# A delta-rule recurrence and an MLP mixer in one kernel: the joins of batch element 0 in 32x32 tiles, with identity products that assemble the blocks in PSUM, and a new order of all steps

## The chip, the core and the metric

The kernel runs on one core of a Trainium2 chip. The metric is the device time of one execution in microseconds (us). The engines are TensorE (PE, with its weight loads PEld), VectorE (DVE), ScalarE (ACT), GpSimd (POOL) and SyncE (SP, which issues all DMAs here). Everything is computed in fp32. Each product of the program shows in the trace as two PE records, except a transpose, which shows as one; counts of records below are therefore mostly twice the counts of products.

## What is computed

```python
# q, k, v: (4, 8, 768, 48), beta: (4, 8, 768)
k_n = k / (norm(k) + 1e-6)
for t in range(768):                       # for each batch element and head
    y[t]  = q[t] @ state                   # state: 48 x 48
    v_old = state @ k_n[t]
    state = state + beta[t] * outer(k_n[t], v[t] - v_old)
x = y as (4, 768, 384)                     # heads side by side
h = relu(x^T @ w_tok1) @ w_tok2            # mixing over the 768 tokens
u = x + h^T
out = u + relu(u @ w_ch1) @ w_ch2          # 384 -> 1536 -> 384
```

## The kernel before, in words

**Units.** The recurrence is done in chunks of 64 time steps (`C`). Two chunks of all 8 heads make a *unit* u of 128 steps; a batch element has 6 units (`NCH`), so there are 24. Units 0 to 5 are batch element 0, and only they take the paths with `u < NCH`. Inside a chunk the steps are solved together, which needs the inverse of a unit triangular 64x64 matrix per head and chunk. A unit holds its eight pairs of them in `gm` (the trace also calls the places of units 0 and 1 `wc`), 128 partitions by 8 blocks (`NB`) of 176 columns; the 64 columns `TC` are the triangular matrix, first as it is and then inverted in place.

**From a unit to its inverse.** `load_kq` (k), `prep` (p) and `grams` (c, d) load k and q, turn them on PE (L488, L507; evicted by ACT at L491, L511) and build the matrices (products L442, DVE L445). `to_parts` (t, L598 on ACT, L603 on DVE, L605 on POOL) copies the diagonal 32x32 blocks of a unit into one tile `xins` for a round of up to four units; `invert` (i) inverts all blocks of a round on DVE. In batch element 0 DVE inverts only the 16x16 diagonal blocks (L676, L680) and then transposes them back twice with 32x32 block transposes: the left 16 columns into `t16` (L686), all of it into `xins` (L693).

**The joins of batch element 0.** Two stages of products make the 64x64 inverse out of 16x16 and 32x32 blocks. `join_16` (h) first forms `p_z` from the untouched matrix and `t16` (L710, 16 products per unit with 64-row, 64-column weights and 32 columns), so that `t16` must hold the blocks of even and of odd quarters in two column halves, with zeros elsewhere: ACT scales a copy by `odd` (L687) and DVE scales it by `even` (L688). ACT evicts `p_z` into `z` in two copies scaled by `sides` (L716). Then `from_parts` (f) writes the inverted diagonal blocks back into `gm`: ACT for all rows, scaled by `even` (L622), DVE (L629) and POOL (L632) for the odd quarters. A second set of 16 products (L725, 48 weight columns) gives the 16x16 corner blocks, which ACT puts in place in four copies of 16 partitions (L731). `join` (j) does the same for 32 to 64: a DVE transpose into `t11` (L749), 16 products (L773), two ACT copies into `zst` (L778), 16 products with 33 weight columns (L760), two ACT copies of 32 partitions into `gm` (L754). The later batch elements go through DRAM and the same `join`, with the second set of products of a unit interleaved with the first set of the next.

**The recurrence.** `recur` (r) has 48 steps, 12 (`NQ`) for each batch element. Step t waits for step t-1 through PE, DVE and ACT: products of the state (L813), DVE subtraction (L820), products (L833, L837), the ACT copy `w_t` (L843), products (L851, L852), the DVE update of the state (L860, first one L862) and the ACT copies of the result into `xb` (L865). Step r0 needs unit 0 joined.

**The mixer.** `mixer` (m) of a batch element begins when its steps are written: token mixing (L1009, L1022), turns (L1032), then the channel MLP in pairs of chunks (L1089 for batch element 0, the faster algorithm L981 with 15 products per pair of blocks for the others, L1111 for the second matrix).

**The order.** The program is recorded under a manual schedule: each function is a generator, and a string `order` of about 2,700 steps (`h0*4` is four steps of `join_16(0)`) says in which order they are recorded. Each engine executes its own instructions strictly in that order. Three kinds of steps are only there to keep PE busy: `x` and `z` multiply zeros by zeros into an unused PSUM tile `p_warm` (128x128 weights and 128 or 512 columns, L227), `y` and `Y` the same in 64x64 tiles (L237).

Of the kernel before, what the change touches and what calls it, by code (L numbers as in the profile page):

```python
# [8 lines left out]
FP32 = mybir.dt.float32  # L9
# [14 lines left out]
def kernel(  # L24
# [508 lines left out]
    for n in (2 * QB * RU * NB,):  # L533
        cuts.append(cuts[-1] + n)
    t16 = spare[:, cuts[1] : cuts[2]].rearrange("s (q t b) -> s q t b", q=2, t=QB)
    borrowed = {}

    def z_of(u):
        if not borrowed:
            borrowed["z"] = mlp_pool.tile(  # L540
                [128, NCH, NB * (C - QB)], FP32, name="z16", tag="xb"
            )
            nc.gpsimd.memset(borrowed["z"], 0.0)
        return borrowed["z"][:, u].rearrange("s (b n) -> s b n", b=NB)
# [7 lines left out]

    even = const.tile([128, 1], FP32, name="even")
    nc.vector.tensor_reduce(
        out=even,
        in_=ident.rearrange("s (q t) -> s q t", t=C)[:, :, 0:HB],
        axis=mybir.AxisListType.XY, op=ALU.add,
    )
    odd = const.tile([128, 1], FP32, name="odd")
    nc.vector.tensor_scalar(  # L560
        out=odd, in0=even, scalar1=-1.0, scalar2=1.0, op0=ALU.mult, op1=ALU.add
    )
    sides = const.tile([128, 2], FP32, name="sides")
    for i, side in enumerate((even, odd)):
        nc.vector.tensor_tensor(
            out=sides[:, i : i + 1], in0=low16, in1=side, op=ALU.mult
        )
# [49 lines left out]
    def from_parts(u):  # L617
        rnd, j = round_of[u]
        assert rnd in turned_back
        if u < NCH:  # L620
            t = xins[rnd]
            nc.scalar.activation(  # L622
                gm_of(u)[:, :, TC.start : TC.start + HB].rearrange("s b t -> s t b"),
                t[:, :, j * NB : j * NB + NB], ACTF.Copy, scale=even,
            )
            inverted.update(((u, 0), (u, 2)))
            yield
            _, (b1, at1, _), _, (b3, at3, _) = quarters(u)
            nc.vector.tensor_copy(out=b1, in_=t[at1].rearrange("s t b -> s b t"))  # L629
            inverted.add((u, 1))  # L630
            yield
            nc.gpsimd.tensor_copy(out=b3, in_=t[at3].rearrange("s t b -> s b t"))  # L632
            inverted.add((u, 3))
            yield
        else:
# [7 lines left out]
    def invert(rnd):  # L643
# [664 lines left out]
```

## Time and profile before

| | |
|---|---|
| median of 3 runs | 645.91 us |
| the runs | 645.91, 651.13 and 644.03 us |
| the profiled execution | 644.78 us, its span 643.0 us |
| PE busy | 614.6 us, 96% |
| DVE, ACT, POOL busy | 446.1, 259.8, 108.9 us |
| mean granted clock of PE | 0.989 |

Busy time is the union of the records of an engine, and ends of products are modelled, so a PE that is 96% busy is not one at its peak; the steps of zeros count as busy. The pitch, from one record's start to the next, tells more about PE than the duration of one record.

### The profile page before, as it was taken

How to read it: one execution, taken by the hardware profiler on the slowest of the kernel's cores; microseconds unless marked ns; L12 is line 12 of the kernel's file. 1: busy time of each engine (PE TensorE's matmuls, PEld its weight loads, DVE VectorE, ACT ScalarE, POOL GpSimd, SP SyncE). 2: the span in 40 equal slices, each digit the busy share in tenths (PEclk: the TensorE clock that was granted, in tenths of full speed). 3: DMA queues.
4: the chain of work that ended last, by engine and by line, in shares of the span. 5: the costliest groups of instructions: out<-in, count | busy, mean ns of one | idle time of the engine just before them, and what ended most of it. 6: DMA issues, size and time to landing. Idle time of an engine off the chain costs nothing. (4 is left out here: it accounts for less than half of the span.)

```text
span 643.0 us, 21493 instructions
## 1 busy us (share of the span) xinstructions
PE 614.6 (96%) x9136; PEld 533.5 (83%) x9136; DVE 446.1 (69%) x1132; ACT 259.8 (40%) x631; POOL 108.9 (17%) x147
## 2 busy tenths in 40 slices
PE   8589899999999999999999999999999999999997
PEld 5358776678888988869899999769999987999997
DVE  4986877978789656988858997685726253373643
ACT  7759787436503332134523332234325140232240
POOL 2446264144200222021200010010020000000000
PEclk9989999999999999999979999999999999999999
DMA  9766667545543454343442222203010000000000
GB/s 192 165 131 156 147 149 199 151 116 131 100 112 76 75 112 107 75 106 70 96 99 68 58 78 44 66 11 53 4 42 4 25 3 0 25 1 25 1 26 25
DMA packets 135776, 50.27 MB, mean 78 GB/s; under 512 B 114656, under 2 KB 130144, under 8 KB 135680
## 3 DMA queue, kind: packets, MB, share of 16 engines
q1 hardware_dynamic: 135680, 48.89, 34.4%
q8 instruction: 72, 1.18, 0.8%
q14 instruction: 24, 0.20, 0.1%
HBM read 39.42 MB, written 9.44 MB: 76 GB/s over the span
## 5 line engine op out<-in xcount | busy, mean ns | idle before, releaser
L1111 PE MATMUL p_o<-wc,r 128*128 128x192 f32 x720 | 128.0, 332 | 0.6 <-ACT u_t L1036 0.6
L1111 PEld LDWEIGHTS p_o<-wc,r 128*128 128x128 f32 x720 | 118.5, 192 | 2.6 <-ACT u_t L1036 1.1
L993 DVE TENSOR_TENSOR r<-r,p_r 128x512 f32<-128x512 f32 x90 | 59.5, 683 | 39.4 <-PE p_r L981 36.9
L1040 DVE TENSOR_TENSOR xb<-xb,p_o 128x192 f32<-128x192 f32 x84 | 29.3, 350 | 57.5 <-PE p_o L1111 57.3
L990 ACT COPY r<-p_r 128x512 f32<-128x512 f32 x54 | 31.3, 584 | 85.9 <-PE p_r L981 78.6
L680 DVE TENSOR_TENSOR x<-x,sub 128x84 f32<-128x84 f32 (+24 forms) x178 | 59.9, 337 | 6.1
L676 DVE TENSOR_TENSOR sub<-x 128x84 f32<-128x84 f32 (+24 forms) x178 | 57.4, 322 | 6.5 <-DMA x<-n_dram 2.3
L1089 PE MATMUL p_c<-u_t,wc 128*128 128x256 f32 x216 | 51.3, 387 | 1.3 <-ACT r L1098 0.7
L1111 PE MATMUL p_o<-wc,s 128*128 128x192 f32 x288 | 51.2, 330 | 0.3 <-DVE xb L1040 0.3
L1111 PEld LDWEIGHTS p_o<-wc,s 128*128 128x128 f32 x288 | 46.8, 190 | 1.2 <-DVE xb L1040 0.6
L1089 PEld LDWEIGHTS p_c<-u_t,wc 128*128 128x128 f32 x216 | 39.6, 190 | 7.4 <-ACT r L1098 1.1
L416 POOL TENSOR_TENSOR v_st<-v_st,nrm 128x384 f32<-128x384 f32 x24 | 20.4, 849 | 148.1 <-DMA v_st<-in_v_dram 66.2
L442 PE MATMUL p_g<-kq 48*64 48x128 f32 (+1 forms) x704 | 38.6, 291 | 6.0 <-ACT kq L511 6.0
L997 ACT ACTIVATE r<-r 128x512 f32<-128x512 f32 x54 | 33.8, 631 | 25.5 <-DVE r L993 25.1
L499 POOL TENSOR_TENSOR mb<-mask_c,cs 128x512 f32<-128x512 f32 x20 | 21.0, 1049 | 129.6 <-DVE cs L478 103.7
L865 ACT ACTIVATE xb<-p_y 64x192 f32<-64x192 f32 x96 | 31.1, 324 | 24.0 <-PE p_y L852 16.3
L981 PE MATMUL p_r<-u_t,wc 128*128 128x128 f32 x288 | 38.6, 277 | 0.0
L981 PE MATMUL p_r<-t_d,wc 128*128 128x128 f32 x288 | 37.6, 281 | 0.0
L843 ACT COPY w_t<-p_w 128x192 f32<-128x192 f32 x48 | 15.3, 318 | 53.2 <-PE p_w L837 52.0
L442 PEld LDWEIGHTS p_g<-kq 48*64 48x64 f32 (+1 forms) x704 | 27.7, 140 | 10.0 <-ACT kq L511 6.8
L981 PEld LDWEIGHTS p_r<-u_t,wc 128*128 128x128 f32 x288 | 35.3, 192 | 0.3
L981 PEld LDWEIGHTS p_r<-t_d,wc 128*128 128x128 f32 x288 | 34.1, 191 | 0.9
(176 smaller groups left out, 1245.3 us busy)
## 6 DMA issues: line engine op xcount, KB each, us to landing
d<-in_moe_w_ch_dram SPq DMA_DIRECT2D x24, 384.0 KB, 3.9
v_st<-in_v_dram SPq DMA_DIRECT2D x96, 48.0 KB, 2.7
out_dram<-xb SPq DMA_DIRECT2D x23, 192.0 KB, 1.9
kst<-in_k_dram SPq DMA_DIRECT2D x64, 48.0 KB, 2.8
n_dram<-gm SPq DMA_DIRECT2D x72, 32.0 KB, 2.1
pads<-in_k_dram SPq DMA_DIRECT2D x24, 96.0 KB, 2.7
pads<-in_q_dram SPq DMA_DIRECT2D x24, 96.0 KB, 2.9
gm<-w_dram SPq DMA_DIRECT2D x72, 32.0 KB, 2.4
```

The costliest lines, as they stand in the source:

```text
L442: nc.tensor.matmul(p_g[PAR[i ^ cc], p], kqt[f, p, cc, 0], kqt[f, p, cc])
L499: scaler.tensor_tensor(out=mb, in0=mask_c[:, None, None, :].to_broadcast([128, NP, 2, C]), in1=cs[:, :, :, None].to_broadcast([128, NP, 2, ...
L676: nc.vector.tensor_tensor(out=tmp, in0=col.to_broadcast(dims), in1=row.to_broadcast(dims), op=ALU.mult,)
L680: nc.vector.tensor_tensor(out=new, in0=new, in1=tmp, op=ALU.add)
L865: nc.scalar.mul(y[:, :, D * i : D * i + D], p_y[PAR[1 - i]], 1.0 if c else -1.0)
L981: nc.tensor.matmul(p[:, i], pieces[i // width][:, at : at + 128], f[f"u{n}"], start=first and i == 0, stop=True, skip_group_check=True,)
L990: nc.scalar.copy(o, p)
L993: nc.vector.tensor_tensor(out=o, in0=o, in1=p, op=ALU.add if sign > 0 else ALU.subtract)
L997: nc.scalar.activation(o, o, ACTF.Relu)
L1040: nc.vector.tensor_tensor(out=xb[:, c, e], in0=xb[:, c, e], in1=p, op=ALU.add)
L1089: nc.tensor.matmul(p_c[:, k], piece_of(wc1, cb, f * 128)[:, f * 128 : (f + 1) * 128], u_t[:, cb], start=(cb == 0), stop=(cb == NCB - 1),)
L1111: nc.tensor.matmul(p, a[:, m], wc2[:, m, j], start=(start and i == 0), stop=(i == NM - 1), skip_group_check=True,)
```

## The change

Four things change; the programs issue the same 512 DMAs.

1. `join_16` works in 32x32 tiles. Its first set is 32 products of 32-row, 32-column weights and 16 columns, straight from `t16`, which is now one transposed copy without the halves. One ACT copy scaled by `low16` evicts `p_z`. The corner products (32 products with 16 weight columns, 16 columns) accumulate in PSUM onto two rounds of four *kept* products: the identity (32x32) times the inverted diagonal blocks out of `xins`, and the identity times the other half of `gm`, 256 columns each. So the whole 64-column block is assembled in PSUM, and one ACT copy of 512 columns puts it into `gm`. `from_parts` is gone for batch element 0, and with it `even`, `odd`, `sides`, the POOL memset of `z`.
2. `join_32` replaces `join` for batch element 0: the first set as before but into the same half, one ACT copy of 256 columns into `z`, two kept products (identity times the odd quarters), 16 products in 32x32 tiles, one ACT copy of 256 columns.
3. There are 35 steps `x` where there were 11: 24 more products of 128 columns of zeros.
4. The string `order` is another one throughout.

```diff
-    t16 = spare[:, cuts[1] : cuts[2]].rearrange("s (q t b) -> s q t b", q=2, t=QB)
+    t16 = spare[:, cuts[1] : cuts[2]].rearrange("s (t b) -> s t b", t=QB)
...
-            nc.vector.transpose(t16[:, 0], x[:, :, 0:QB].rearrange("b t s -> b s t"))
-            nc.scalar.activation(t16[:, 1], t16[:, 0], ACTF.Copy, scale=odd)
-            nc.vector.tensor_scalar(
-                out=t16[:, 0], in0=t16[:, 0], scalar1=even, scalar2=None, op0=ALU.mult
-            )
+            nc.vector.transpose(t16, x[:, :, 0:QB].rearrange("b t s -> b s t"))
...
+    QUADS = [slice(HB * i, HB * i + HB) for i in range(4)]
+
+    def kept(p, r, rhs, start):
+
+        nc.tensor.matmul(
+            p[r], ident[r, r], rhs[r], start=start, stop=False, skip_group_check=True
+        )
+
     def join_16(u):
...
-        p_z = ps_prep([128, NB, 2, QB], "p_z")
+        p_z = ps_prep([128, NB, QB], "p_z")
         for nb in range(NB):
-            for r in PAR:
-                nc.tensor.matmul(p_z[r, nb], wt[r, nb], t16[r, :, :, j * NB + nb])
+            for i, r in enumerate(QUADS):
+                cols = QUADS[i % 2]
+                nc.tensor.matmul(p_z[r, nb], wt[r, nb, cols], t16[r, :, j * NB + nb])
...
-        for i in range(2):
-            nc.scalar.activation(
-                z[:, :, HB * i : HB * i + QB], p_z[:, :, i], ACTF.Copy,
-                scale=sides[:, i : i + 1],
-            )
+        nc.scalar.activation(z, p_z, ACTF.Copy, scale=low16)
         yield
-        assert inverted.issuperset((u, i) for i in range(4))
-        p_x = ps_prep([128, NB, C - QB], "p_x")
+        d = xins[rnd][:, :, j * NB : j * NB + NB].rearrange("s t b -> s b t")
+        p_x = ps_prep([128, NB, C], "p_x")
+        for i, r in enumerate(QUADS):
+            kept(p_x[:, :, QUADS[i % 2]], r, d, True)
+        for i, r in enumerate(QUADS):
+            kept(p_x[:, :, QUADS[1 - i % 2]], r, wt[:, :, QUADS[1 - i % 2]], False)
         for nb in range(NB):
-            for r in PAR:
+            for i, r in enumerate(QUADS):
+                at = HB * (i % 2) + QB
                 nc.tensor.matmul(
-                    p_x[r.start : r.stop - QB, nb], z[r, nb], wt[r, nb, QB:C]
+                    p_x[r.start : r.start + QB, nb, at : at + QB], z[r, nb],
+                    d[r, nb, QB:HB], start=False, stop=nb == NB - 1,
+                    skip_group_check=True,
                 )
...
-        for i, (block, _, _) in enumerate(quarters(u)):
-            nc.scalar.copy(
-                block[0:QB, :, QB:HB],
-                p_x[HB * i : HB * i + QB, :, HB * (i % 2) : HB * (i % 2) + QB],
-            )
-            joined_16.add((u, i))
-            yield
+        nc.scalar.copy(wt, p_x)
+        joined_16.add(u)
+        yield
+
+    def join_32(u):
...
+        nc.vector.transpose(t11, wt[:, :, 0:HB])
...
+                nc.tensor.matmul(p_z[r, nb], wt[r, nb], t11[r, nb])
...
+        nc.scalar.copy(z, p_z)
+        yield
+        p_x = ps_prep([128, NB, HB], "p_x")
+        for r in QUADS[1::2]:
+            kept(p_x, r, wt[:, :, HB:C], True)
+        for nb in range(NB):
+            for k in range(2):
+                e, o = QUADS[2 * k], QUADS[2 * k + 1]
+                nc.tensor.matmul(p_x[e, nb], z[o, nb], wt[o, nb, HB:C])
...
+        nc.scalar.copy(wt[:, :, HB:C], p_x)
...
     order = """
-    w10 z w10*2 z k1 z b k0 k1*2 b z x k1*2 k3 k0 z k1 k0*2 p1*2 k0 w2 k0 p0*2 b p1
+    w10*2 z k1 b z w10 k0 z k1*2 k0 z k1*3 p1 k0*3 k3 w2 p1 k0 b p0 p1 p0 b p0*2
...
```

Where the new order and the new joins meet, the engines' rows read as follows. PE from the first join on, before (`r_130` is the tile that holds `t16` and `xins`, `wc_127` and `gm` the matrices, `z_581` the evicted `p_z`; the size is that of the output):

```order
L710 MATMUL p_z<-r_130,wc_127 64x32 x32
L227 MATMUL p_warm<-warm 128x512
L725 MATMUL p_x<-wc_127,z_581 48x48 x16
L710 MATMUL p_z<-r_130,gm 64x32 x16
L227 MATMUL p_warm<-warm 128x512
L773 MATMUL p_z<-t_108,wc_127 64x32 x16
L725 MATMUL p_x<-wc_127,z_581 48x48 x16
L760 MATMUL p_x<-wc_127,zst 33x32 x16
```

The same place after, with the kept products on `ident` (L667) and the lines of the new program:

```order
L682 MATMUL p_z<-r_130,wc_127 32x16 x56
L227 MATMUL p_warm<-warm 128x128
L682 MATMUL p_z<-r_130,wc_127 32x16 x8
L667 MATMUL p_x<-r_130,ident 32x8x32 x4
L667 MATMUL p_x<-wc_127,ident 32x8x32 x4
L699 MATMUL p_x<-r_130,z_559 16x16 x32
L682 MATMUL p_z<-r_130,gm 32x16 x32
L667 MATMUL p_x<-r_130,ident 32x8x32 x4
L667 MATMUL p_x<-wc_127,ident 32x8x32 x4
L699 MATMUL p_x<-r_130,z_559 16x16 x32
L720 MATMUL p_z<-t_108,wc_127 64x32 x16
```

So the two long products of zeros between the joins have become one short one, unit 1's `join_16` now stands whole ahead of unit 0's second stage, and unit 2's first set has stayed between them. ACT at the same place, before, from the copy by `odd` to the last copy ahead of r0's `w_t`:

```order
L716 ACTIVATE z_581<-p_z,sides 128x8x16 x4
L622 ACTIVATE wc_127<-r_130,even 128x32x8
L465 ACTIVATE ksq<-kst_94 128x384
L622 ACTIVATE wc_127<-r_130,even 128x32x8
L731 COPY wc_127<-p_x 16x8x16 x4
L622 ACTIVATE gm<-r_130,even 128x32x8
L716 ACTIVATE z_581<-p_z,sides 128x8x16 x2
L279 ACTIVATE d_687<-d_687 128x256
L280 ACTIVATE d_687<-d_687 128x256
L778 COPY zst<-p_z 32x256 x2
L731 COPY wc_127<-p_x 16x8x16 x4
L754 COPY wc_127<-p_x 32x8x32 x2
```

and after, where L687 evicts `p_z` of `join_16`, L706 puts the assembled block into the matrix, and L723 and L734 are the two copies of `join_32`:

```order
L706 COPY wc_127<-p_x 128x8x64
L687 ACTIVATE z_559<-p_z,low_131 128x128
L465 ACTIVATE ksq<-kst_93 128x384
L581 COPY r_130<-gm 128x32x8
L279 ACTIVATE d_775<-d_775 128x384
L280 ACTIVATE d_775<-d_775 128x384
L706 COPY wc_127<-p_x 128x8x64
L723 COPY z_559<-p_z 128x256
L279 ACTIVATE d_806<-d_806 128x256
L280 ACTIVATE d_806<-d_806 128x256
L491 COPY kq_98<-p_t 128x4x128
L734 COPY wc_127<-p_x 128x8x32
```

Twenty-one instructions of the joins have become five in these rows (with two more L687 ahead of them), and the pairs L279 and L280 that round a piece of the weights have moved in between. The third place is PE in step r31, in the recurrence of batch element 2, between its products `p_w` and `p_s`. Before, the turns of the mixer stand there, and no product of zeros stands anywhere after r11:

```order
L833 MATMUL p_y<-s_t_114,kq_97 64x48
L837 MATMUL p_w<-rest,gm 64x48
L1032 MATMUL p_ut<-ident,xb 128x128 x6
L851 MATMUL p_s<-w_t,gm 64x48
L852 MATMUL p_y<-w_t,gm 64x48
```

After, half of the turns stand there, behind the last of the new products of zeros:

```order
L832 MATMUL p_y<-s_t_114,kq_97 64x48
L836 MATMUL p_w<-rest,gm 64x48
L227 MATMUL p_warm<-warm 128x128
L1031 MATMUL p_ut<-ident,xb 128x128 x3
L850 MATMUL p_s<-w_t,gm 64x48
L851 MATMUL p_y<-w_t,gm 64x48
```

The other half of the turns has moved ahead of `p_w`, and one product of zeros came in.

More of the change, by code (lines that the diff above doesn't have):

```diff
@@ L551 @@
     )
[L553 to L557, printed above, removed]
-    )
-    odd = const.tile([128, 1], FP32, name="odd")
-    nc.vector.tensor_scalar(
-        out=odd, in0=even, scalar1=-1.0, scalar2=1.0, op0=ALU.mult, op1=ALU.add
-    )
[L563 to L566, printed above, removed]
-        )
     def turned_of(rnd):
@@ L619, in from_parts @@
         assert rnd in turned_back
[L620 to L624, printed above, removed]
+        for i, (block, _, rows) in enumerate(quarters(u)):
+            nc.sync.dma_start(
+                out=block, in_=xouts[rnd][rows].rearrange("b s t -> s b t")
             )
[L626 removed]
+            inverted.add((u, i))
             yield
[L628 to L641 removed]
     def invert(rnd):
@@ L786, in join @@
             return
-        assert done.issuperset([(u, 1), (u, 3)])
+        assert inverted.issuperset([(u, 1), (u, 3)])
         p_x = ps_prep([128, NB, HB], "p_x")
```

238 lines of the change are left out of this document (127 added, 111 removed).

## The prediction

> **What bounds the kernel now.** The page's table of busy time comes first, then its slices.
>
> ```profile
> PE 614.6 (96%) x9136; PEld 533.5 (83%) x9136; DVE 446.1 (69%) x1132; ACT 259.8 (40%) x631; POOL 108.9 (17%) x147
> ...
> PEclk9989999999999999999979999999999999999999
> ```
>
> PE is the bound on the average, and its clock drops twice: early, and in the 21st slice. The table of windows, cut where the stages change, shows where PE is the bound. Columns: start:end, length, then busy time and instructions of PE, PEld, DVE, ACT and POOL, the granted clock, DMA share, GB/s.
>
> ```profile
> 28.00:39.00 11.00, 7.01 (x45) 4.49 (x46) 9.97 (x34) 3.76 (x9) 5.36 (x6) 0.69 0.89 198
> 39.00:54.00 15.00, 12.64 (x292) 9.32 (x292) 10.41 (x20) 12.35 (x34) 8.89 (x12) 1.00 0.44 97
> 54.00:121.00 67.00, 60.60 (x1676) 49.07 (x1676) 54.80 (x142) 50.40 (x137) 32.69 (x40) 1.00 0.71 168
> 121.00:324.00 203.00, 198.52 (x3260) 167.14 (x3260) 161.64 (x403) 76.37 (x196) 40.12 (x51) 1.00 0.45 99
> 324.00:331.00 7.00, 7.00 (x76) 6.91 (x69) 4.82 (x17) 0.65 (x2) 0.00 (x0) 0.55 0.33 51
> 331.00:520.00 189.00, 188.31 (x2762) 172.07 (x2761) 126.08 (x333) 63.42 (x147) 12.47 (x20) 1.00 0.20 44
> ```
>
> The same windows for `p_warm` alone, the products of zeros (PE, PEld):
>
> ```profile
> 39.00:54.00 15.00, 4.09 (x10) 1.20 (x8) 1.00 0.44 97
> 54.00:121.00 67.00, 6.98 (x44) 3.55 (x44) 1.00 0.71 168
> 121.00:324.00 203.00, 1.47 (x6) 0.83 (x6) 1.00 0.45 99
> ```
>
> From 121 us on PE does needed work almost without a gap: 4.5 us idle of 203, 0.7 of 189. Whatever shortens that part must take work off PE or keep its clock up. Before 121 us PE is no bound: in 28 to 39 us DVE is busy 9.97 of 11 us with the inversion, in 39 to 54 ACT 12.35 of 15, and in 54 to 121 PE, DVE and ACT share the load, with 6.4 us of PE idle and 7.0 of zeros. The chain there is read from three rows of the timeline: the transpose that ends the first inversion, the first ACT instruction behind it, and the `w_t` copies of r0 and r11.
>
> ```profile
> 39.45 1.06 DVE L686 STREAM_TRANSPOSE r<-x 128x512 f32<-128x512 f32 x1
> 40.54 0.72 ACT L687 ACTIVATE r<-r,odd 128x512 f32<-128x512 f32 x1 [2.86 <-DVE r L686]
> 53.71 0.34 ACT L843 COPY w_t<-p_w 128x192 f32<-128x192 f32 x1
> 121.06 0.32 ACT L843 COPY w_t<-p_w 128x192 f32<-128x192 f32 x1
> ```
>
> The first joins take 14.3 us from the transpose to r0, the eleven steps from r0 to r11 67.4 us. Only when batch element 0 is near its end is there mixer work enough to fill PE. So the time is about the time of r11 plus the PE work that is left.
>
> **What the change does on ACT and DVE.** The groups of the joins, all of them ahead of r11 or close to it:
>
> ```profile
> L731 ACT COPY gm<-p_x 16x128 f32<-16x128 f32 x16 | 4.1, 254 | 0.2
> L731 ACT COPY wc<-p_x 16x128 f32<-16x128 f32 x8 | 2.1, 256 | 0.3 <-PE p_x L725 0.2
> L716 ACT ACTIVATE z<-p_z,sides 128x128 f32<-128x128 f32 x12 | 3.7, 364 | 1.4 <-PE p_z L710 1.3
> L622 ACT ACTIVATE gm<-r,even 128x256 f32<-128x256 f32 x4 | 3.0, 739 | 0.0
> L622 ACT ACTIVATE wc<-r,even 128x256 f32<-128x256 f32 x2 | 1.5, 738 | 0.0
> L778 ACT COPY zst<-p_z 32x256 f32<-32x256 f32 x12 | 4.4, 364 | 1.2 <-PE p_z L773 1.0
> L754 ACT COPY gm<-p_x 32x256 f32<-32x256 f32 x8 | 2.9, 358 | 0.1
> L754 ACT COPY wc<-p_x 32x256 f32<-32x256 f32 x4 | 1.4, 358 | 0.1
> L687 ACT ACTIVATE r<-r,odd 128x512 f32<-128x512 f32 x2 | 1.4, 722 | 3.0 <-DVE r L686 2.9
> L629 DVE COPY gm<-r 32x256 f32<-32x256 f32 x4 | 2.3, 564 | 0.8 <-PE p_z L710 0.7
> L629 DVE COPY wc<-r 32x256 f32<-32x256 f32 x2 | 1.5, 728 | 0.1
> L688 DVE TENSOR_SCALAR r<-r,even 128x512 f32<-128x512 f32 x2 | 1.0, 486 | 1.6 <-ACT r L687 1.6
> L491 ACT COPY kq<-p_t 128x512 f32<-128x512 f32 x9 | 5.2, 578 | 0.8 <-PE p_t L488 0.7
> ```
>
> ACT loses 4.1+2.1+3.7+3.0+1.5+4.4+2.9+1.4+1.4 = 24.5 us. It gains, for each of six units, one copy like L716 (0.36), one of 512 columns out of PSUM like L491 (0.58) and two of 256 columns, which I put at L778's 0.36 since that has the same columns: 6 x 1.66 = 10.0 us. Net 14.5 us off ACT. DVE loses 2.3+1.5+1.0 = 4.8 us. POOL (idle 6 of the 15 us and half of the 67) loses its copies L632 and a memset; I cost that at nothing, since ACT's longer copies beside it covered them.
>
> **What it does on PE.** The pitches of the short products, from three rows of the timeline (second column is the length from the first start to the last end):
>
> ```profile
> 46.12 1.12 PE L710 MATMUL p_z<-r,gm 64*64 64x32 f32 x32
> 45.39 0.92 PE L725 MATMUL p_x<-wc,z 64*48 64x48 f32 x32 [0.34 <-issue]
> 50.35 0.71 PE L760 MATMUL p_x<-wc,zst 64*33 64x32 f32 x32 [0.47 <-ACT zst L778]
> 11.96 1.15 PE L442 MATMUL p_g<-wc 64*64 64x128 f32 x32 [0.24 <-ACT wc L511]
> L1089 PE MATMUL p_c<-u_t,wc 128*128 128x256 f32 x216 | 51.3, 387 | 1.3 <-ACT r L1098 0.7 <-ACT u_t L1036 0.6
> ```
>
> With some 0.2 us off for the last record's own length, a record comes every 29 ns with 64 weight columns, every 23 with 48 and every 17 with 33: the pitch goes with the weight columns, two tiles being at work side by side. The new 32-column products have 64 records in a set where there were 32. Between 8.5 ns (four tiles side by side) and 17 (no gain from four), a set costs 0.5 to 1.1 us, where it was 0.93 and 0.74; I take 0.8, nearest to L760 without its full price. A kept product has 256 columns in two records: side by side in four tiles it costs between 0.06 us (L442's 28 ns for 128 columns with two tiles, doubled for the columns, halved for four tiles, two records) and 0.47 (L1089's 237 ns a record, one after another). I take 0.1, because L442, a short-tile product, is the nearer row: ten for each unit are 1.0 us. A unit then costs about 1 us more on PE, six units 6 us (from -2 to +30 at the ends). In 39 to 54 us the two long products of zeros that went (L227, some 0.8 us each) cover two units' share; in 54 to 121 the 6.4 us of idle cover four units' 4 us.
>
> **The terms.** The sums along the orders add the durations of before's groups, instruction by instruction. (1) r0. Ahead of the inversion's end the new order leaves DVE 1.9 us less to do (the masks' constants and some rounding of weights and evictions are gone from there). From the transpose to r0 ACT bounds (12.35 of 15 us busy); its new rows there add up to 8.8 us, so ACT alone would give back 4. PE becomes the next late one: its rows there come to 10 to 13 us. Together 2.3 to 5.1 us; I take 4.0. (2) r0 to r11: DVE has 3.5 us less ahead of r11's copy than before, ACT 8 less, PE 6 to 9 more (3 to 4 of it zeros). If DVE decides it is 3.5, if PE decides 0; I take 2.5. (3) The clock. In 324 to 331 us it was 0.55, and PE had no idle: 7 x 0.45 = 3.2 us lost. The stretch before it has short products and idle PE, and that is where the order now puts a product of zeros and splits the turns of r31. I take the drop as gone, ends 0 and 3.2. (4) Eleven of the new products of zeros stand behind r11 where PE is full. A 128-column product is two records of 0.134 us (38.6/288):
>
> ```profile
> L981 PE MATMUL p_r<-u_t,wc 128*128 128x128 f32 x288 | 38.6, 277 | 0.0
> ```
>
> That is 3.0 us at most, and 0 if all fall into the 5 us of idle; I take 3.0. The other thirteen stand ahead of r11 beside idle PE, cost nothing while that lasts, and 0.27 each if the joins use it up. (5) SP issues the same 512 DMAs, but a weight piece, a k load and a part of v now go ahead of the fourth q load: 0.64 MB, 3.2 us at the 198 GB/s of the first window above. Its issue before, the time to landing of its kind, and the turn that needs it:
>
> ```profile
> 9.15 1.89 SPq L385 DMA_DIRECT2D lent<-in_q_dram  x1
> ```
>
> ```profile
> lent<-in_q_dram SPq DMA_DIRECT2D x6, 192.0 KB, 4.5
> ```
>
> ```profile
> 21.02 0.60 PE L507 MATMUL p_t<-ident,lent 128*128 128x128 f32 x4
> ```
>
> It landed by about 16 and was needed at 21 us, so 5 us of slack cover 3.2; I take 0. Without the slack, 3 us on r0.
>
> The execution shown took 644.8 us: 644.8 - 4.0 - 2.5 - 3.2 + 3.0 = 638.1. That run lies 1.1 us under the median 645.9, so the gain against the median is 1.2%; 1% is about what a measurement of this kernel can tell from no change, and the runs shown differ by more.
>
> **A rule against it.** The rows for the change from 128-row to 64-row tiles:
>
> ```profile
> 144.38 0.60 PE L488 MATMUL p_t<-ident,lent 128*128 128x128 f32 x4
> 144.91 0.62 PE L837 MATMUL p_w<-v_st,gm 64*64 64x48 f32 x13
> ```
>
> Four transposes at a pitch of 0.11 leave their next slot at 144.81; the other tiles begin 0.10 later. The order has 255 changes of tile size where it had 234, so 21 x 0.10 = 2.1 us, in the idle of the first part. The Trainium skill, TensorE: Matmul & The Clock Gate (Back-to-back issue gap), puts a floor of about 25 ns under the distance of two matmuls, however few their columns. By it the short sets would cost 1.6 us instead of 0.8, an estimate by that page; the trace does not agree, L760 has 17 ns.
>
> **The rivals.** (A) *A floor under the short tiles*: records of 16 and 32 columns come no faster than L710's 29 ns. Two sets of 64 records are 1.9 us each where they were 0.9 and 0.7: with `join_32` about 2.4 us more for each unit, 14 in all, of which the idle covers half: 644 or 645. L760's 17 ns speaks against it, though no row has a 32-row tile. The floor of that page would be this case. (B) *Kept products one after another, PE the bound of the first part*: ten at 0.47 are 4.7 us a unit; two units put r0 5 us later instead of 4 earlier, four add 19 less 6.4 of idle: 644.8 + 5 + 12 - 3.2 + 3.0 = 662 at the full price, 655 at two thirds. It decides from about 0.22 us a product, where four units' forty products eat the idle and DVE's 2.5. The strided reading of `xins` speaks for it, L442's pitch against. (C) *The gain is eaten*: the clock falls at another place (the runs of 644 to 651 us differ by about such drops) and r11 comes only 3 us earlier: 644.8 - 3.3 + 3.0 = 644.5. (D) *All ends good*: r0 5.1 and r11 3.5 earlier, zeros in idle, clock up: 644.8 - 5.1 - 3.5 - 3.2 = 633.0, less if the early clock at 0.69 also stays up.
>
> **The numbers.** Forecast 0.48, of which 0.42 below 639.5 us (1% under the median) and 0.06 above, its own range 633 to 643; D 0.13, below; C 0.16 and A 0.06, within 1%; B 0.17, slower. So faster 0.55, same 0.28, slower 0.17. The range from 630 to 652 leaves out B and the end of D.
>
> **What would show it.** r0's `w_t` copy near 49.7 us (52 or later: term 1 wrong), r11's near 114.5 (over 121: B); the kept products of a unit within 1.0 us; ACT's busy time 14 us less; PEclk without a drop behind the 10th slice; PE idle after r11 under 8 us. The forecast is wrong if the kept products don't run side by side, or if the clock falls again.

## The result, and the profile after

The changed kernel takes 664.47 us (median of 4 runs, 662.31 to 667.49) where the kernel before, on the same chip, takes 646.58 (4 runs, 644.03 to 651.13): a ratio of 1.027, with a 95% interval of 1.022 to 1.032. The forecast was 638.0 in a range of 630 to 652. The execution profiled took 662.87 us, its span is 661.1.

The page of after, busy time and clock, against the two lines that open the prediction:

```profile
PE 630.0 (95%) x9688; PEld 544.8 (82%) x9688; DVE 437.3 (66%) x1120; ACT 246.0 (37%) x587; POOL 102.4 (15%) x140
...
PEclk9998879999999998999899999999999999999999
```

ACT has 13.8 us less to do (259.8 before) and DVE 8.8, as the change meant, and PE has 15.4 us more. The clock, once a dip of one slice behind the early one, is below 9 in the 4th to 6th slice, the 16th and the 20th. The windows cut at the `w_t` copies of r0 and r11 show where the time went (columns as in the prediction). Before:

```profile
0.00:53.70 53.70, 40.92 (x566) 27.30 (x566) 39.29 (x105) 38.76 (x99) 23.31 (x37) 0.94 0.81 157
53.70:121.10 67.40, 60.82 (x1676) 49.19 (x1676) 54.90 (x142) 50.75 (x139) 32.99 (x40) 1.00 0.72 169
121.10:643.00 521.90, 512.88 (x6896) 456.98 (x6894) 351.89 (x886) 170.29 (x395) 52.59 (x71) 0.99 0.26 58
```

After:

```profile
0.00:55.70 55.70, 45.39 (x818) 30.72 (x820) 35.72 (x101) 34.00 (x86) 20.73 (x35) 0.91 0.85 165
55.70:128.60 72.90, 66.02 (x1954) 52.08 (x1954) 48.29 (x133) 40.79 (x105) 27.01 (x32) 0.93 0.59 141
128.60:661.10 532.50, 518.58 (x6931) 462.01 (x6920) 353.33 (x886) 171.25 (x397) 54.65 (x73) 0.99 0.25 58
```

r0 is 2.0 us later instead of 4.0 earlier, r11 7.5 later instead of 6.5 earlier, and the stretch behind r11, where only zeros were to be paid, is 10.6 us longer. Two things are to be explained, then: the part ahead of r11 (the *head*), where DVE and ACT have a tenth and a sixth less to do and nothing came of it, and the part behind (the *tail*), where the joins play no part.

**The head.** PE in the first joins, after (start, length from the first start to the last end, count of records):

```profile
41.42 1.04 PE L667 MATMUL p_x<-r,ident 32*32 32x256 f32 x8
42.26 0.64 PE L667 MATMUL p_x<-wc,ident 32*32 32x256 f32 x8
...
44.00 0.77 PE L682 MATMUL p_z<-r,gm 32*32 32x16 f32 x64
...
48.00 1.92 PE L720 MATMUL p_z<-t,wc 64*64 64x32 f32 x32
49.85 1.11 PE L488 MATMUL p_t<-ident,pads 128*128 128x128 f32 x4
```

From the first start to the next row's, the four kept products that read `xins` with a stride take 0.84 us, 0.21 each, and the four on the contiguous matrix 0.45, 0.11 each. The short set of 64 records takes 0.77, less 0.2 for the last record's own length a pitch of 9 ns. At 48 us the clock is at half: four transposes take 1.11 us where the prediction's row has 0.60. The tile `p_x` as a whole, PE alone, before and after:

```profile
39.00:54.00 15.00, 3.80 (x128) 1.00 0.44 97
54.00:121.00 67.00, 7.09 (x256) 1.00 0.71 168
```

```profile
39.00:54.00 15.00, 6.57 (x211) 0.77 0.57 128
54.00:121.00 67.00, 11.98 (x492) 0.92 0.60 143
```

So 7.7 us more of PE went into the joins ahead of 121 us, part of it at half clock.

**The tail.** ACT's square of k, `ksq` (L465), between 121 and 400 us, before and after (busy, mean ns, then idle time just before it and what ended it):

```profile
L465 ACT ACTIVATE ksq<-kst 128x384 f32<-128x384 f32 x12 | 6.3, 522 | 7.3 <-DMA kst<-in_k_dram 5.2 <-issue 2.1
```

```profile
L465 ACT ACTIVATE ksq<-kst 128x384 f32<-128x384 f32 x12 | 6.3, 522 | 29.7 <-DMA kst<-in_k_dram 27.2 <-issue 2.5
```

ACT now stands 27 us in front of k loads that have not landed. One such place, by engine: SP's issues, ACT, and PE.

```profile
314.29 0.60 SPq L403 DMA_DIRECT2D v_st<-in_v_dram  x1
314.93 1.43 SPq L359 DMA_DIRECT2D pads<-in_k_dram  x2
316.77 1.26 SPq L403 DMA_DIRECT2D kst<-in_k_dram  x2
318.09 0.61 SPq L595 DMA_DIRECT2D n_dram<-gm  x1
318.74 2.59 SPq L403 DMA_DIRECT2D kst<-in_k_dram  x2
```

```profile
323.08 0.52 ACT L465 ACTIVATE ksq<-kst 128x384 f32<-128x384 f32 x1 [4.35 <-DMA kst<-in_k_dram]
...
324.85 0.66 ACT L864 ACTIVATE xb<-p_y 64x192 f32<-64x192 f32 x2
```

```profile
325.57 0.31 PE L832 MATMUL p_y<-s_t,kq 48*64 48x48 f32 x2 [2.21 <-ACT xb L864]
```

SP issues one DMA after the other, the last piece of `kst` by 321.3; ACT's square waits for it 4.35 us, the copy into `xb` stands behind the square, PE's next `p_y` needs the PSUM that this copy frees, and PE is idle for 2.21 us. The clock falls there, and so it does from 258 us on, where PE waits for DVE's turn L368 and that for a late q load. PE's waits behind r11, by what it waited for (us, times, longest), in after:

```profile
PE p_g L442 <- DVE kq L368: 3.3, 3, 2.0
PE p_y L832 <- ACT xb L864: 2.6, 2, 2.2
PE p_s L850 <- ACT w_t L842: 2.4, 3, 1.2
```

The longest of these in before:

```profile
PE p_w L837 <- DVE rest L820: 1.4, 3, 0.8
```

### The profile page after: what moved, and what is told of

Read it like the earlier page. It is cut to its first block, busy times and chain, and to the rows that moved or that the text cites. A ratio compares the mean times of both kernels' runs of the same rounds, so it can differ in the third digit from the quotient of the medians.

```text
span 661.1 us, 22538 instructions
## 1 busy us (share of the span) xinstructions
PE 630.0 (95%) x9688; PEld 544.8 (82%) x9688; DVE 437.3 (66%) x1120; ACT 246.0 (37%) x587; POOL 102.4 (15%) x140
## 4 chain that ended last, share of the span: by engine, by line
PE 72%; SPq 8%; DVE 8%; DMA 5%; ACT 3%; issue 3%; DVEq 0%; ACTq 0%
PE p_o L1110 19%; PE p_r L980 17%; PE p L1008 5%; PE p_h L1021 5%; PE p_c L1088 4%; PE p_g L442 3%; SPq L403 3%; PE p_s L850 2%; PE p_k L812 2%; SPq L359 2%; PE p_y L832 2%; SPq L595 2%; PE p_warm L227 2%; SPq L604 2%; PE p_x L667 1%
## 5 line engine op out<-in xcount | busy, mean ns | idle before, releaser
L1110 PEld LDWEIGHTS p_o<-wc,r 128*128 128x128 f32 x720 | 116.7, 190 | 3.1 <-ACT u_t L1035 1.1
L1088 PEld LDWEIGHTS p_c<-u_t,wc 128*128 128x128 f32 x216 | 41.3, 197 | 6.0
L996 ACT ACTIVATE r<-r 128x512 f32<-128x512 f32 x54 | 33.9, 631 | 27.5 <-DVE r L992 27.2
L980 PE MATMUL p_r<-t_d,wc 128*128 128x128 f32 x288 | 39.0, 285 | 0.0
```

The lines of the kernel that those rows point to most:

```text
L980: nc.tensor.matmul(p[:, i], pieces[i // width][:, at : at + 128], f[f"u{n}"], start=first and i == 0, stop=True, skip_group_check=True,)
L996: nc.scalar.activation(o, o, ACTF.Relu)
L1088: nc.tensor.matmul(p_c[:, k], piece_of(wc1, cb, f * 128)[:, f * 128 : (f + 1) * 128], u_t[:, cb], start=(cb == 0), stop=(cb == NCB - 1),)
L1110: nc.tensor.matmul(p, a[:, m], wc2[:, m, j], start=(start and i == 0), stop=(i == NM - 1), skip_group_check=True,)
```

## The experiments

Every execution has its span and its mean granted clock, so each kernel's span splits in two: span times clock, the time that it would take at full clock if all of it went with the clock, and the rest, lost to the clock. The table has the mean of both over the executions of each kernel (62 of before, 4 to 12 of the others); the executions of one kernel spread by 0.9 to 4.0 us (one standard deviation) in the first of the two. Changes are read against before, or against after where the text says so. The diffs of the order are cut to some of the lines that change, with the line breaks of before or after.

| run | median us | ratio to before (95%) | full clock | lost |
|---|---|---|---|---|
| before | 646 | 1 | 637.1 | 7.2 |
| after | 664.47 | 1.027 (1.022 to 1.032) | 646.3 | 16.6 |
| e1_new_joins_old_order | 652.21 | 1.010 (1.006 to 1.015) | 640.1 | 10.4 |
| e2_old_joins_new_order | 665.45 | 1.030 (1.026 to 1.034) | 647.7 | 16.1 |
| e3_11_zeros | 664.67 | 1.028 (1.023 to 1.033) | 645.0 | 17.9 |
| e4_long_zeros | 671.79 | 1.040 (1.036 to 1.044) | 661.8 | 8.2 |
| e5_old_head_new_tail | 658.06 | 1.018 (1.014 to 1.022) | 644.9 | 11.3 |
| e6_joins_short_zeros | 647.20 | 1.004 (1.001 to 1.007) | 635.6 | 10.0 |
| e7_kept_twice | 662.45 | 1.025 (1.021 to 1.030) | 653.4 | 7.6 |
| e8_new_head_old_tail | 654.82 | 1.012 (1.007 to 1.016) | 637.8 | 14.9 |
| e9_k_loads_early | 666.20 | 1.033 (1.029 to 1.038) | 647.5 | 15.0 |
| e10_kq_loads_early | 669.72 | 1.036 (1.030 to 1.042) | 650.2 | 17.0 |
| e11_join_32_alone | 643.95 | 0.997 (0.994 to 1.000) | 634.8 | 7.8 |
| e12_v_loads_on_pool | 657.80 | 1.018 (1.013 to 1.024) | 641.9 | 14.3 |
| e13_before_v_on_pool | 653.29 | 1.013 (1.006 to 1.020) | 641.1 | 10.6 |
| e14_new_from_r24 | 651.82 | 1.008 (1.005 to 1.011) | 642.2 | 7.5 |
| e15_square_on_pool | 666.69 | 1.032 (1.027 to 1.038) | 646.4 | 19.0 |
| e16_v_on_pool_no_late_zeros | 659.14 | 1.020 (1.015 to 1.024) | 644.3 | 13.0 |
| e17_join_32_again | 643.81 | 0.997 (0.994 to 1.000) | 634.9 | 7.5 |

So by the table the 18.6 us of after against before are half work and waits (9.2), half clock (9.4). The split is rough. Among the executions of one kernel (161 in all), an execution that lost 1 us more of clock took only 0.64 us longer (least squares), as if part of a stretch at half clock were covered by waits, so "full clock" comes out too low for a kernel that lost much. At 0.64, an estimate from these executions, the 18.6 us are 12.6 of work and waits and 6.0 of clock.

### Joins, order, zeros

The first four kernels take the parts of the change one by one. e1 is the program of after with the steps in the old order (less the steps that the new joins do not have):

```diff
-    w10*2 z k1 b z w10 k0 z k1*2 k0 z k1*3 p1 k0*3 k3 w2 p1 k0 b p0 p1 p0 b p0*2
+    w10 z w10*2 z k1 z b k0 k1*2 b z x k1*2 k3 k0 z k1 k0*2 p1*2 k0 w2 k0 p0*2 b p1
...
```

> The joins of after under the order of before (the steps of the removed copies left out, 11 products x). Theory K, the 32-row tiles of the joins let the granted clock of PE fall and that costs the time: half clock again in more than the two spells of before, around the joins, r0 no earlier than 53 us, time 652 to 660. Theory O, the new order costs the time and the joins are good: r0 near 50, r11 near 115 us, time 636 to 642. Theory Z, the 24 products of zeros cost it: the same as O.

e2 is the opposite: the program of before in the new order, with the steps f0 to f5 and the last three of h0 to h5 put in where the old joins need them.

> The joins of before under the order of after (the copies of the inverted blocks put just ahead of the second set of products, 35 products x). Theory K: clock as in before, two spells at half, r11 near 121 us, time 646 to 652. Theory O: slower than before by all or most of the 2.7%, 658 to 668, r12 to r24 some 7 us longer than before. Theory Z: 24 x 0.27 = 6 us more than before, 652.

e3 is after with only the first eleven of its 35 short products of zeros, none of them behind r1; e4 is after with all 35 four times as long, every `x` of the order a `z`:

```diff
-    k2 x p0 w13 w10 p0 p1 p0*2 p1 p0 k2 k4 d0 w2 v0 k3 p1 c0 w2 k2 d0 k2 c0 k2 p0
+    k2 z p0 w13 w10 p0 p1 p0*2 p1 p0 k2 k4 d0 w2 v0 k3 p1 c0 w2 k2 d0 k2 c0 k2 p0
...
```

> After with its first 11 products x alone, as many as before has (none behind r1). Theory Z: 658. Theory K: the clock has still less to hold it, spells at half of 30 us or more in all, 662 to 670. Theory O: 659 to 664, the zeros on full PE alone come off (13 x 0.27 = 3.5 us).

> After with every x (128 columns of zeros) made a z (512 columns). That is 35 x about 0.5 us more of zeros. Theory K: the clock falls less often in the first 121 us (spells at half under 15 us in all), which gives back up to 8 us and costs about 7 behind r11 where PE is full: 660 to 666. Theories O and Z: clock or not, 668 to 680.

The order alone, with the old joins, costs all that the change costs (1.030), the joins alone in the old order a third of it (1.010): theory O for the larger part. But the joins are not good by themselves, as O has it: e1's 652.2 is K's figure, where O expected 636 to 642, and the two losses do not add up. Z falls: without the 24 products the time is the same. Their place is taken by idle time and lost clock (17.9). Four times as long they hold the clock (8.2 us lost instead of 16.6), as K expected, but take 15.5 us themselves, and the time is that of O and Z. K holds in part only: the clock falls with the new joins, but in e2 it falls as much with the old ones.

### Where the order costs

e5 keeps before up to r11 and has the new order from there on; e8 keeps after up to r11 and has the old order from there on; e14 is like e5 with the cut at r23. In each, what is left behind the cut follows in the second order, without the steps done already.

> The kernel before with its old joins and its old order up to and with step r11; what is left follows in the new order. Theory T (the new order behind r11 costs by itself: 5 us more of idle PE, 3 to 4 us of zeros): r11 stays at 121 and the span grows by the difference of the stretches behind r11, 661.1 - 128.6 against 643.0 - 121.1, so 10 us: 654 to 658 us. Rival H (the loss behind r11 is a late legacy of the first part: loads and turns that stand behind it): 645 to 649 us.

> The kernel after, with the new joins and the new order up to and with step r11; what is left follows in the old order, with none of the new products of zeros behind r11. Theory T: r11 at 128 to 130 as in after, the stretch behind it as in before, 522 us of span: 650 to 654 us. Rival H (the loss behind r11 comes from the first part): 660 to 664 us.

> The kernel before with old joins and its old order up to and with step r23; what is left follows in the new order. If the loss behind r11 is spread evenly over batch elements 1 and 2, as the steps say (7.5 us from r12 to r24 and 3.6 from r24 to r36 in after, of which lost clock is 3.4 more in the first), 4 to 6 us are lost: 650 to 652 us. If it is one place ahead of r24 that costs, 645 to 648 us; if one place behind it, 655 to 658.

The windows of e5 and of e8, from r11 to the end:

```profile
126.40:657.40 531.00, 514.87 (x6914) 459.36 (x6912) 352.68 (x886) 170.06 (x395) 52.65 (x70) 1.00 0.25 57
```

```profile
133.80:653.30 519.50, 510.03 (x6914) 453.81 (x6905) 350.81 (x885) 171.29 (x397) 54.06 (x73) 1.00 0.26 59
```

The stretch goes with its own order, whatever the head was: 531.0 in the new, 519.5 in the old. Theory T, and H falls. By the table the kernel with the new tail (e5) loses 7.8 us at full clock and 4.1 of clock, the one with the new head and its joins (e8) 0.7 at full clock and 7.7 of clock. Of the tail's loss 5.1 us remain when only r24 and later are new (e14), so it is spread over both batch elements.

The traces place the clock differently. Behind r11 the half clock loses 2.1 us in e5 and 5.2 in after, against 3.5 in before and nothing in e8; the other 8.6 us that e5's execution lost were lost ahead of r11, in before's own program. That the new tail costs 4.1 us of clock is therefore not shown; most of what it costs is time at full clock, 528.9 and 527.3 us in e5 and after against 518.4 and 519.5 in before and e8. A good part of that is idle PE: counted from record to record, PE waits 13.2 and 10.9 us behind r11 in e5 and after, 6.1 and 6.3 in before and e8.

### The head: PE's work and its clock

e6 is before with one edit, the two long products of zeros between the first joins made short:

```diff
-    k5*2 h1*2 k8 h1*2 h0 h1 w17 z f0*3 h0 w8*2 p3 v1 h0 p5 f1*3 k8 h0*3 v1 v0 h0*2
-    v0 h2*3 t4 h2 h0 z f2 h2 w0*2 j0 w11 j0 w6 j0*4 k5 h1*6 j0*3 h1*2 f2*2 j1 p5 t4
+    k5*2 h1*2 k8 h1*2 h0 h1 w17 x f0*3 h0 w8*2 p3 v1 h0 p5 f1*3 k8 h0*3 v1 v0 h0*2
+    v0 h2*3 t4 h2 h0 x f2 h2 w0*2 j0 w11 j0 w6 j0*4 k5 h1*6 j0*3 h1*2 f2*2 j1 p5 t4
```

> The kernel before, with one edit: the two long products of zeros between the first joins (512 columns, at 43.9 and 47.2 us) are of 128 columns. Theory C (these two hold the clock through the joins): the clock halves between 42 and 60 us for 7 to 17 us, r0 comes 3 us or more later than 53.7, r11 5 us or more later than 121: 650 to 655 us. Rival N (the clock there hangs on something else): r0 0.5 to 1 us earlier, 645 to 646 us.

e7 is after with the first kept products issued twice:

```diff
-        nc.tensor.matmul(
-            p[r], ident[r, r], rhs[r], start=start, stop=False, skip_group_check=True
-        )
+        for _ in range(2 if start else 1):
+            nc.tensor.matmul(
+                p[r], ident[r, r], rhs[r], start=start, stop=False, skip_group_check=True
+            )
```

> The kernel after, with the first kept products of each set issued twice, over the same output: six more per unit, four that read with a stride (0.84 us by the trace of after) and two that don't (0.23), 1.07 us for a unit and 6.4 for the six. Theory P (PE's work in the first part adds to the time as it is, nothing covers it): r11 5 to 7 us later than 128.6, 669 to 671 us. Rival I, the prediction's own assumption (idle PE and waits on ACT and DVE cover it): r11 within 2 us, 664 to 666 us.

e6's window of the joins, to be read beside the prediction's 39 to 54 us of before, with its clock of 1.00:

```profile
39.00:54.00 15.00, 13.41 (x232) 10.72 (x232) 9.44 (x21) 9.36 (x25) 8.72 (x12) 0.71 0.44 106
```

The shorter zeros give 1.5 us back and lose 2.8 to the clock: C in direction, at less than its price, and a net loss of 0.4%. In this execution r11 is at 126.8 us, the 5 us later that C asked for, but that is no sign for C, because the profile of before was a lucky one: the identical first part put r11 at 121.1 us there and at 126.4, 125.3 and 126.2 in e5, e13 and e14, as the clock fell.

The same luck bears on the head as a whole. Four profiles have before's program up to r11 (before, e5, e13, e14) and reach it at 124.7 us on the mean; five have after's (after, e8, e12, e15, e16) and reach it at 128.6 to 133.8 us, 131.2 on the mean. So the new head is 6.4 us later, and 3.7 of these are lost clock (10.5 us instead of 6.9).

The windows of e7 up to r11:

```profile
0.00:55.20 55.20, 44.98 (x846) 28.46 (x848) 35.60 (x101) 33.55 (x85) 20.75 (x35) 0.97 0.87 167
55.20:131.90 76.70, 71.47 (x1998) 54.85 (x1998) 48.59 (x135) 40.71 (x106) 27.04 (x32) 0.93 0.56 135
```

At full clock (length times clock of both rows) r11 is at 124.9 us, where after has 118.5: 6.4 later, all of P's price. But in this measure the five profiles with after's head, which have no doubled products, scatter from 118.5 (after) to 123.5 (e16), so this trace alone does not decide. Over the executions the kernel's full-clock time is 7.1 us longer than that of after, or 3.9 at equal lost clock by the 0.64 above. So part of P's price is paid, by this estimate more than half, and theory I, the prediction's, that idle PE covers it, does not hold in full; that nothing is covered is not shown. The time itself did not grow, since 9.0 us of lost clock came back with the products. Neither number was hit, because the expectation left the clock out.

### The tail: SP's queue

e9 moves the four `kst` loads of units 12 to 23 ahead in the new order, as far as their buffer allows (43 loads moved, 1 to 38 steps); e10 moves the q loads as well.

> The kernel after, with one kind of step moved: the four loads of k into kst of units 12 to 23, which SP issues, stand as far ahead as the buffers allow, 1 to 38 steps earlier than before; nothing else moves. Theory S (behind r11 the new order issues these loads too late, ACT's square L465 stands waiting for them, and the copies behind it on ACT make PE wait): ACT's idle time ahead of L465 falls from 27 us to under 10, PE's idle time behind r11 from 11 us to 6 to 8, the stretch behind r11 is 3 to 6 us shorter: 657 to 661 us. Rival W (the loss lies in the order of PE's own products): ACT's idle time falls, the time stays at 663 to 667 us.

> As the run with the k loads early, and the four loads of q of units 13 to 23 go ahead as well, up to 98 steps. Theory S: the waits of DVE's turn L368 for these loads (3.0 us, and 3.3 us of PE idle behind them) go too, 1 to 3 us less than with the k loads alone: 655 to 660 us. Rival W: 663 to 667 us. A third way, SP full: the loads of v and the blocks n_dram and w_dram that are now behind them on SP become the late ones, and the time is that of the run with k alone or more.

Neither helped. In e9 ACT's idle time ahead of the square fell from 27.2 to 20.0 us, not to 10, and the time is that of after; in e10 it is 21.3 and the median is 5 us above that of after, which is the third way of the expectation. DVE's waits from 125 to 500 us, in e10 and in after, tell where e10's loads went (us, times, longest):

```profile
DVE sub L643 <- DMA x<-n_dram: 16.9, 3, 6.3
```

```profile
DVE sub L643 <- DMA x<-n_dram: 5.0, 2, 2.7
```

What is moved ahead on SP delays what stood there, here the blocks for the next inversion. SP is not full, though. Of the 275 us from 125 to 400 us its issues take 193 in after and 195 in before. What grew is the time that SP itself stands in front of the stores of `out` (L1042, in before L1043), which wait for DVE: 37.0 us in all instead of 25.6. The longest groups, in after and in before:

```profile
SPq L1042 <- DVE sub L643: 31.1, 6, 15.3
```

```profile
SPq L1043 <- DVE xb L1040: 13.6, 1, 13.6
SPq L1043 <- DVE sub L676: 11.1, 5, 7.0
```

The waits ahead of `w_dram` (L659, in before L696) grew as well, from 14.4 to 21.0 us. A load that stands behind such a place waits with it, and the two orders differ in this whatever the joins are (38.5 us ahead of the stores in e2, 23.1 in e1). No run moves the stores. So e12 takes work off SP and leaves the order: the v loads of units 12 to 23 are issued by POOL. e13 does the same in before, as a control, and e15 leaves the loads and takes the square off ACT.

```diff
-    def stacked(dst, src, u):
+    def stacked(dst, src, u, queue=nc.sync):
...
-                nc.sync.dma_start(
+                queue.dma_start(
...
-        yield from stacked(v_st, v, u)
+        yield from stacked(v_st, v, u, nc.gpsimd if u >= TU else nc.sync)
```

> The kernel after, with the 48 loads of v of units 12 to 23 issued by POOL instead of SP; the order of the steps is unchanged. Theory Q (SP's queue as a whole is late behind r11, whatever stands first in it): with 48 issues of 0.45 to 0.6 us less on SP, ACT's wait ahead of L465 falls from 27 us to under 12, PE's idle time behind r11 from 11 us to under 8, and the time is 657 to 661 us. Rival W (the waits come from the order of the products and of ACT's and DVE's rows, the queue would be in time for another order): 663 to 667 us.

> The control: the kernel before with the same 48 loads issued by POOL. Theories Q and W both expect no change here, 644 to 648 us, since ACT waits 5 us for these loads in before and PE not at all. More than that would say that a load issued by POOL has a price of its own, to be taken off the run with the kernel after.

```diff
-        nc.scalar.square(ksq, kst.rearrange("s p c d -> s (p c) d"))
+        flat = kst.rearrange("s p c d -> s (p c) d")
+        if u < TU:
+            nc.scalar.square(ksq, flat)
+        else:
+            nc.gpsimd.tensor_tensor(out=ksq, in0=flat, in1=flat, op=ALU.mult)
```

> The kernel after, with the square of k of units 12 to 23 (ksq, L465) computed by POOL instead of ACT, so that ACT no longer stands waiting for kst; the loads and the order are unchanged. Theory B (ACT's in-order queue behind the waiting square is what makes PE wait): PE's waits for ACT's xb and w_t fall from 5.0 us to under 2.5, the time is 658 to 662 us. Rival D (whoever waits, the unit itself comes late, and PE waits for its products p_g through DVE): p_g's waits stay or grow, 663 to 667 us.

PE's waits behind r11 in e12:

```profile
PE p_s L850 <- ACT w_t L842: 1.9, 2, 1.4
PE p_y L832 <- ACT xb L864: 1.4, 2, 1.0
PE p_g L442 <- DVE kq L368: 1.2, 2, 0.8
```

The same edit makes after 6.7 us faster and before 6.9 slower (against the 646.43 beside it; both theories expected 644 to 648), so loads that are late behind others on SP are part of what the new tail suffers from: theory Q. PE's idle time behind r11 falls to 6.9 us, as Q expected; the 2.0 us wait at 258 us and the drop of the clock behind it are gone, although ACT's wait for `kst` fell to 19.5 us only, not under 12. Whether the queue is late because of the number of its issues or because of what SP stands waiting for, e12 does not tell. In e15 ACT no longer waits there, and the waits move: PE then waits 4.6 us for DVE's `rest` (L823) and the time stays. B's time is not met. But POOL, which now stands in front of the same loads (17.8 us at the longest), also scales v, and the sign of D, longer waits of `p_g`, did not come (1.0 us instead of 3.3). That the late unit and not the queue of the waiting engine costs is argued, not shown.

e16 takes the eleven products of zeros behind r11 out of e12:

> The kernel after with the v loads on POOL, and without the eleven products of 128 columns of zeros behind r11. Theory Z2 (zeros cost nothing only while PE waits for loads anyway; with the loads in time they cost their own 3 us): 2 to 4 us less than the run with the v loads on POOL alone, 654 to 656 us. Rival G (they hold the clock, or still stand in idle time): 657 to 660 us.

No gain: PE is idle where the zeros stood, 10.1 us behind r11 instead of 6.9. Z2's 2 to 4 us did not come, though the two intervals (1.013 to 1.024 and 1.015 to 1.024) would let 2 us pass unseen. What the rest of the tail's loss is (full clock 641.9 in e12, 4.8 over before) stays open; e12's edit acts only from 245 us on, where POOL issues its first v load, and the waits ahead of that are unchanged. That a POOL load costs the same 4 us in both kernels, so that SP's share would be about 8 us, is argued from e13 and not shown.

### A part that costs nothing

e11 is before, in its old order, with the old `join_16` and the new `join_32`, and e17 is the same kernel, measured more often:

```diff
-        jobs[f"j{u}"] = join(u)
+        jobs[f"j{u}"] = join_32(u) if u < NCH else join(u)
```

> The kernel before in its old order, with the old join_16 and the new join_32 alone. Theory J (the price on PE lies in join_16, with its eight kept products, four of them read with a stride): p_x takes 1 to 2 us more of PE ahead of r11 instead of 8 to 10, ACT 4 to 5 us less, the time is 643 to 648 us. Rival K (any set of products in 32-row tiles lets the clock fall): half clock ahead of r11 for 20 us or more, as with both new joins in the old order, and 650 to 653 us.

> The same kernel as the run with the new join_32 alone in the old order, with more rounds, since its ratio of 0.997 (0.994 to 1.000) left open whether it is faster than before. If join_32 gains what it takes off ACT: ratio 0.995 to 0.998 with an interval below 1. If it was the luck of the runs: 0.998 to 1.002.

Both runs give 0.997, the second with an interval of 0.9942 to 0.9999: 2 us faster than before, the only version here that is. Theory J: the windows of e17 show a clock nearly as high as in before, `p_x` takes 11.5 us of PE up to 121 us where before has 10.9, and ACT has 4.4 us less over the whole span (255.4).

```profile
0.00:54.70 54.70, 42.50 (x570) 28.44 (x570) 39.25 (x105) 37.85 (x97) 23.14 (x37) 0.91 0.79 153
54.70:123.40 68.70, 61.63 (x1696) 49.82 (x1696) 54.65 (x142) 47.20 (x128) 33.12 (x40) 1.00 0.69 167
```

## Why the prediction was wrong

The miss is 664.5 - 638.0 = 26.5 us. The steps, in the prediction's order, with the splits of the table (at 0.64 us for each us of lost clock the shares of clock are smaller and those of work larger):

- **The prices.** ACT's net 14.5 us came as 13.8. The short sets, put at 0.8 us, took 0.77 at full clock (rival A's floor is not there: 9 ns a record). The kept products, put at 0.1 us, cost 0.21 with the strided read and 0.11 without (that it is the stride that costs is read from these rows; no run changes it alone). A unit's ten are 1.5 us instead of 1.0. Rival B saw the strided read; its limit of 0.22 was nearly met by those four, but its mechanism, products one after another at 0.47, did not come.
- **Terms 1 and 2, the cover. This step failed.** The long products of zeros that went were to "cover two units' share", and the idle PE of 54 to 121 us the other four. The head gained 6.5 us in the forecast, and e8 has 0.7 us of loss at full clock: 7.2 us of the miss. ACT did give back its share (7.77 us busy instead of 12.35 in 39 to 54 us), and r0 came later all the same. That the 7.7 us more on `p_x` ate the gain fits e7, where added products cost part of their price, but how much of it was covered stays open.
- **The same zeros and the clock. This failed too.** They were counted as free slots, and the clock of the head was put at nothing. e6 shows that the two long ones also keep the clock up. With them gone, in the new order and with the joins in small tiles, the kernel with the new head loses 7.7 us more to the clock than before (e8). Either part does it alone: ahead of r11 the profile of e2 (order) loses 13.6 us of clock and that of e1 (joins) 15.4, those with before's program 6.9 on the mean. Rival C named a falling clock and priced it at the late drop's 3.2.
- **Term 3.** The late drop was to go, a gain of 3.2. In after the clock in 324 to 331 us is 0.76 instead of 0.55, but a drop at 258 came in, behind a wait of PE for a late load. Nor does the drop come with the old order: the profiles of e1, e6, e8 and e17, which keep that order behind r11, have no half clock between 135 and 630 us. As far as these show, it was the luck of the one execution that the forecast was read from, and there was no 3.2 us to gain.
- **Term 4.** The zeros behind r11 were sized somewhat low (`p_warm` keeps PE busy there for 6.72 us against 1.47, 36 records against 6), but they stand where PE would be idle, and no cost of theirs shows (e3, e16).
- **Term 5, SP. This is the step that failed most.** It asked whether one load at the start, with 5 us of slack, becomes late, and took 0. Behind r11 no load's time against its use was looked at, on the ground that the issues are the same 512. The kernel with the new tail loses 7.8 us at full clock and 4.1 of clock (e5), where the forecast had -0.2 (zeros +3.0, drop -3.2): 12.1 us of the miss. Taking the v loads off SP gives 6.7 us of it back (e12), or more if a load on POOL has a price of its own (e13); the rest is open.

The three sums, 7.2, 7.7 and 12.1, make 27.0 for the 26.5; that they come out so close is luck in part, since each is uncertain by 1 to 2 us. Of the signs named ahead, r0 past 52, r11 past 121, clock drops behind the 10th slice, kept products of over 1.0 us a unit (1.5) and PE idle of over 8 us behind r11 (10.9, counted from record to record) all spoke against the forecast, and only ACT's busy time spoke for it.

## What to carry to other kernels

When an order is rewritten, go through the in-order DMA queue first: for every load, compare the time of its issue with the instruction that waits for it, see what stands behind that instruction, and see for which engine the queue itself stands waiting. A share of busy time below one does not mean that an engine has slots to give: in a serial chain part of the work that it gains is paid, however idle the profile's page calls it. In this kernel products of zeros are part of the clock's budget: making two of them short lost more in clock than the work saved (e6), and the joins in small tiles alone lost 10.4 us of clock instead of 7.2 (e1). And a single execution is no base for a term of the clock: see in a second one whether the drop is there again.

## What the runs showed of the hardware

- Products in 32x32 tiles with 32 weight columns and 16 columns come every 9 ns, four tiles at work.
- The kept products that read their moving operand with a stride take 0.21 us each (256 fp32 columns, two records, four tiles side by side), those that read it contiguously 0.11.
- The clock falls with PE busy. In 39 to 54 us of after PE is busy 12.75 of 15 us, and the clock is 0.77:

```profile
39.00:54.00 15.00, 12.75 (x445) 9.62 (x449) 7.49 (x18) 7.77 (x20) 7.99 (x11) 0.77 0.57 128
```

In the traces' record of the clock it is full or half, and the stretches at half last 3.4 us or a multiple (6.8 from 47 us here). The Trainium skill, TensorE: Matmul & The Clock Gate (What's actually happening), has such a gate, which decides in free-running windows of 3.4 us on how busy PE was. The trace agrees, and a window that runs free of the program fits the 5 us by which r11 of one and the same program moved. The Trainium skill's advice on the same page (Why this matters for your kernels), no idle gaps over about 3 us, was not enough here: the longest gap of PE between 41 and 54 us was 1.00 us, among small tiles.
